# Attention into two MLP blocks on one core: P V of two heads in 128x64 tiles, row sums by their own products

## The chip, the core and the metric

The kernel runs on one core of a Trainium2 chip. TensorE (PE) does the products, VectorE (DVE) and ScalarE (ACT) the elementwise work, GpSimd (POOL) one reduction, and SyncE's queue (SP) issues the transfers. The metric is device time in microseconds (us); lower is better.

## The reference, cut to what is computed

```python
# q, k, v: 4 batches x 8 heads x 576 positions x 64
scores = scale * rotate(q) @ rotate(k).T
attn = exp(scores - max(scores)) ; attn /= sum(attn) + 1e-9
x = concat_heads(attn @ v)                                # 4 x 576 x 512
x = x + relu((x - mu) / sqrt(var + 1e-6) * g_ln @ w_ch1) @ w_ch2      # 512 -> 2048 -> 512
h = gelu(x @ w_in) ; u, v = split(h)                      # the second block
out = x + (u * (w_sg @ layernorm(v) + b_sg)) @ w_out
```

## The kernel before

All is float32. Products of weights and activations are split into a high and a low half and done as three single-pass products (`F32R`); P V, and the products with a matrix of ones, are done as plain `F32`, which the trace shows as two weight loads and two passes for each product.

**Attention** (class `Attn`) works in 64 units: 4 batches, 4 pairs of heads, 2 halves of 288 queries, 2 heads. A pair of heads of one half is a block (32 of them). Keys lie on the 128 partitions in 5 chunks, queries in the 288 columns. One unit (`unit`, L325) goes: scores S (10 products, L333) into the one five-bank PSUM tile; a maximum over the chunks on DVE (`mx`, L356); a maximum over the partitions on POOL (`am`, L359); then either `add` (L414: five products on PE add the negative maximum to S, and ACT takes the exponential out of PSUM) or `subtract` (L398: DVE subtracts from PSUM into SBUF, ACT takes the exponential there). P lies in `sT`, of which there are `SB` = 2. Then P V (L372, in the one PSUM bank `PV`): the stationary tile of 128 columns is 64 columns of V and 64 columns of ones, so one product gives P V in one half of the partitions and the row sums of P in the other. ACT copies both out (L379, L382), and a transfer brings one row of sums to `sums`. The first 31 units add; from the moment all 32 weight tiles are converted (`spare`, L485) every unit subtracts.

**Between and after**: `ln` (L495) divides by the sums and normalises when a batch's units are through; `rest` (L539) splits the result into `xh` and `xl`; `up` (L666) and `down` (L693) are the first MLP in four groups, one for each batch, 768 products a group; `moe2` (L923) is the second block. The 32 MLP weight tiles come as 8-byte values and are converted on ACT and DVE (`convert`, L636) during the first units.

**Order**: `Sched` (L61) places every step of every engine at build time, in a list for each engine, from a table of planned durations and ranks; the chip then runs these lists strictly in order, and only semaphores hold an engine up. So the table of durations decides the order and not the time.

Of the kernel before, what the change touches and what calls it, by code (L numbers as in the profile page):

```python
# [15 lines left out]
NC5 = 5  # L16
HQ = 288
SB, QB, KB, AB = 2, 3, 4, 1
WB, WX, CB = 8, 3, 4
KC = (0, 256, 576)  # L20
KEY0 = (0, 128, 256, 384, 448)
L_CONV = 10.0
HOLD = 0.4
UNIT = (0, 2.5, 2.5, 2.5)
# [107 lines left out]
class Attn:  # L132
# [10 lines left out]
    def __init__(self, tc, ctx, k, groups, sched):  # L143
# [7 lines left out]
        self.vin = [self.p.tile([128, NC5, 192], F32, tag=f"vin{i}", name=f"vin{i}", bufs=1) for i in range(2)]  # L151
        self.sums = [self.p.tile([64, HQ], F32, tag=f"sums{i}", name=f"sums{i}", bufs=1) for i in range(3)]
        self.last = {}
        self.done = []
        self.blocks, self.units = [], []
        for g, (b, halves) in enumerate(groups):
# [4 lines left out]
            for n, (hi, p) in enumerate(order):  # L161
# [6 lines left out]
                B["vof"]["users"] = B["vof"].get("users", 0) + 2  # L168
                B["kof"]["kusers"] = B["kof"].get("kusers", 0) + 2
                for j in range(2):  # L170
                    ends = j == 1 and (n == 7 or (g == 0 and n == 3))
                    self.units.append(dict(i=len(self.units), B=B, g=g, p=p, hi=hi, j=j, ends=ends))
# [38 lines left out]
    def first(self):  # L211
# [8 lines left out]
        t = self.p.tile([128, NC5, HQ], F32, tag="sT", name="q0", bufs=SB)  # L220
        self.sT.take()
# [27 lines left out]
    def prep(self, bi):  # L249
# [54 lines left out]
        if B["newk"]:  # L304
            c.task(k_task(), 3.01 + 0.02 * bi)
        c.task(*((q_twice(), 3.035) if bi == 1 else (q_task(), 3 + 0.02 * bi)))

    def load_v(self, bi):
        nc, B = self.nc, self.blocks[bi]

        def v_task():
            e = yield "SP", self.vfree.free, 0.7
            slot = B["vslot"] = self.vfree.take()
            t = B["vin"] = self.vin[slot]
            for j in range(2):
                if j:
                    e = yield "SP", 0.0, 0.7
                nc.sync.dma_start(out=t[:, :, 128 * j:128 * j + 64], in_=self.k["v"][B["b"], B["p"]][:, :, j, :])
            B["v"] = e + 5.5

        if B["newv"]:
            self.c.task(v_task(), 3.03 + 0.02 * bi)


    def unit(self, i):  # L325
# [34 lines left out]
        if self.k["spare"]():  # L360
# [3 lines left out]
        V = B["vof"]  # L364
        ps = None
        for c0, c1 in ((0, 2), (2, 5)):
            e = yield "PE", (lambda: latest(x1, self.PV.free(), V["v"])) if c0 == 0 else 0.0, 0.51 * (c1 - c0), 0.5
# [9 lines left out]
        a, b = 64 * j, 64 - 64 * j  # L377
        yield "ACT", e + 0.35, 0.41
        nc.scalar.copy(self.k["x0"](g, p, hi)[a:a + 64], ps[a:a + 64])  # L379
        e = yield "ACT", 0.0, 0.41  # L380
        t = self.p.tile([128, HQ], F32, tag="sr", name="sr", bufs=1)
        nc.scalar.copy(t[b:b + 32], ps[b:b + 32])  # L382
        self.PV.give(bank, e + 0.1)
        e = yield "SP", e + 0.1, 0.6
        r = 32 * hi + 2 * p + j
        nc.sync.dma_start(out=self.sums[self.sums_of(g, hi)][r:r + 1], in_=t[b:b + 1])
        if u["ends"]:
            self.done.append(e + 3.0)

    def new_sT(self):  # L390
        return self.sT.take(), self.p.tile([128, NC5, HQ], F32, tag="sT", name="sT", bufs=SB)

    def subtract(self, am, at):
# [7 lines left out]
        for c0, c1 in ((0, 2), (2, 5)):  # L401
            e = yield "ACT", e + 0.1 if c0 == 0 else 0.0, 0.1 + 0.29 * (c1 - c0)
# [3 lines left out]
    def add(self, am, at):  # L406
# [5 lines left out]
        for c0, c1 in ((0, 2), (2, 5)):  # L412
# [8 lines left out]
        c.e["ACT"] = max(c.e["ACT"], e + 0.35) + 0.89  # L421
# [24 lines left out]
def fused_kernel(ctx, tc, q, k, v, cs, cst, w12, wi, wo, wsg, wsg4, gb, out):  # L446
# [13 lines left out]
    ones = const.tile([128, 128], F32, name="ones")  # L460
    gbt = const.tile([128, 2, 4], F32, name="gbt")
# [23 lines left out]
    attn = Attn(tc, attn_ctx, dict(q=q, k=k, v=v, cs=csb, e=e128, x0=get_x0, x0_free=x0_free, spare=lambda: stored[0] == 32), groups, C)  # L485
# [9 lines left out]
    def ln(g, his, at):  # L495
        n = len(his)
        yield "DVE", at, 0.3
# [9 lines left out]
        for hi in his:  # L507
# [29 lines left out]
            C.task(rest(g, hi, his, st, xc, t, xn[0], e + 0.1), 2)  # L537
# [623 lines left out]
```

## Time and profile before

| | us |
|---|---|
| runs: median (lowest to highest of 3) | 973.72 (972.16 to 974.61) |
| profiled execution: span, first to last instruction | 970.5 |
| PE busy, products / weight loads | 924.1 / 857.2 |
| DVE busy | 705.4 |
| ACT busy | 470.0 |
| POOL busy | 87.8 |

The profiled execution is listed with its span alone; the runs lie 1.7 to 4.1 us above it, the median 3.2 us. The engines run side by side, so the busy times don't add up to the span. Products are pipelined on PE: a record lasts longer than the distance to the next one, and the cost of a product is the distance of two starts, not the length of the record.

### The profile page before, as it was taken

The numbers are of one execution on the slowest core, as the hardware profiler recorded it, in microseconds if no ns is written. First come the engines' busy times: TensorE is split into PE (matmuls) and PEld (weight loads), VectorE is DVE, ScalarE is ACT, GpSimd is POOL, SyncE is SP. The second block draws the span as 40 slices with busy tenths as digits, with TensorE's granted clock in tenths as the row PEclk, the third lists the DMA queues.
The fourth block names the chain that finished last, engine by engine and source line by source line (L and its number), as shares of the span: only waits on it lengthen the run. The fifth ranks groups of instructions, "written<-read, shape, count | busy, mean of one in ns | idle before, by whom it ended". The sixth has DMA issues, their size and how long they took to land.

```text
span 970.5 us, 15810 instructions
## 1 busy us (share of the span) xinstructions
PE 924.1 (95%) x6027; PEld 857.2 (88%) x6027; DVE 705.4 (73%) x1153; ACT 470.0 (48%) x946; POOL 87.8 (9%) x78
## 2 busy tenths in 40 slices
PE   4777899999999899999999999999999999999998
PEld 3555788999999789999989999999999999989998
DVE  6988766898878997678888744675543798677764
ACT  3666657776532464444245532525422467254431
POOL 1221111101110112120012110000000000000000
PEclk9998999999999999999999999999999999999999
DMA  8798733898537086564763723698753300303011
GB/s 228 207 276 269 222 85 87 249 333 279 185 126 217 14 209 188 163 196 119 237 185 92 221 92 110 221 301 259 245 194 110 92 8 12 98 1 93 1 49 50
DMA packets 93404, 153.47 MB, mean 158 GB/s; under 512 B 38032, under 2 KB 60816, under 8 KB 93328
## 3 DMA queue, kind: packets, MB, share of 16 engines
q1 hardware_dynamic: 92784, 151.86, 50.9%
q8 instruction: 48, 0.79, 0.3%
q10 hardware_dynamic: 544, 0.59, 0.2%
q14 instruction: 28, 0.23, 0.1%
HBM read 107.55 MB, written 26.21 MB: 138 GB/s over the span
## 4 chain that ended last, share of the span: by engine, by line
PE 81%; DVE 11%; DMA 3%; ACT 3%; issue 2%; POOL 1%; SPq 0%; DVEq 0%; ACTq 0%
PE PV L372 12%; PE S L333 7%; PE m L708 7%; PE m L707 7%; PE m L709 7%; PE m L677 6%; PE m L679 5%; PE m L678 5%; DVE mx L356 2%; DMA sums<-sr 2%; PE p L1072 2%; PE p L1070 2%; PE p L1071 2%; PE p L989 2%; PE p L988 2%; PE p L1087 2%
## 5 line engine op out<-in xcount | busy, mean ns | idle before, releaser
L372 PE MATMUL PV<-sT,vin 128*128 128x288 f32 x640 | 167.6, 409 | 1.1 <-ACT sr L382 0.9
L677 PE MATMUL m<-xh,w 128*128 128x288 f32 x480 | 147.8, 308 | 3.2 <-DVE h L687 3.2
L372 PEld LDWEIGHTS PV<-sT,vin 128*128 128x128 f32 x640 | 118.6, 191 | 29.0 <-ACT sr L382 1.4
L707 PE MATMUL m<-h,w 128*128 128x288 f32 x480 | 144.3, 301 | 0.0
L678 PE MATMUL m<-xl,w 128*128 128x288 f32 x480 | 142.6, 297 | 1.0 <-DVE xl L550 1.0
L679 PE MATMUL m<-xh,w 128*128 128x288 f32 x480 | 141.9, 296 | 0.0
L708 PE MATMUL m<-h,w 128*128 128x288 f32 x480 | 141.8, 296 | 0.0
L709 PE MATMUL m<-h,w 128*128 128x288 f32 x480 | 140.7, 293 | 0.0
L356 DVE TENSOR_REDUCE mx<-S 128x288 f32<-128x1440 f32 x64 | 105.9, 1655 | 39.6 <-PE S L333 37.2
L359 POOL PARTITION_ALL_REDUCE am<-mx x64 | 85.7, 1338 | 487.0 <-DVE mx L356 487.0
L333 PE MATMUL S<-X,K 128*128 128x288 f32 x640 | 111.8, 315 | 16.9 <-ACT X L202 9.6
L333 PEld LDWEIGHTS S<-X,K 128*128 128x128 f32 x640 | 93.4, 195 | 27.7 <-ACT sT L417 10.7
L687 DVE SCALAR_TENSOR_TENSOR h<-m,h 128x288 fp32r<-128x288 f32 x128 | 58.1, 454 | 63.9 <-ACT h L685 63.1
L685 ACT ACTIVATE h<-m 128x288 fp32r<-128x288 f32 x128 | 52.6, 411 | 98.8 <-PE m L679 98.0
L677 PEld LDWEIGHTS m<-xh,w 128*128 128x128 f32 x480 | 90.7, 189 | 7.3 <-DVE h L687 4.7
L678 PEld LDWEIGHTS m<-xl,w 128*128 128x128 f32 x480 | 90.9, 189 | 2.7 <-DVE xl L550 1.5
L707 PEld LDWEIGHTS m<-h,w 128*128 128x128 f32 x480 | 90.1, 188 | 1.2 <-DVE h L687 0.2
L708 PEld LDWEIGHTS m<-h,w 128*128 128x128 f32 x480 | 90.2, 188 | 1.0
L679 PEld LDWEIGHTS m<-xh,w 128*128 128x128 f32 x480 | 91.0, 190 | 0.0
L709 PEld LDWEIGHTS m<-h,w 128*128 128x128 f32 x480 | 90.1, 188 | 0.0
L379 ACT COPY x<-PV 64x288 f32<-64x288 f32 x64 | 25.2, 394 | 93.1 <-PE PV L372 92.6
L403 ACT ACTIVATE sT<-sT 128x576 f32<-128x576 f32 x66 | 50.9, 801 | 31.2 <-DVE sT L398 31.1
(151 smaller groups left out, 1855.7 us busy)
## 6 DMA issues: line engine op xcount, KB each, us to landing
w<-wsc SPq DMA_DIRECT2D x96, 512.0 KB, 4.5
X<-qin SPq DMA_DIRECT2D x120, 144.0 KB, 2.6
cd<-in_w SPq DMA_DIRECT2D x32, 512.0 KB, 5.9
wsc<-w SPq DMA_DIRECT2D x24, 512.0 KB, 4.4
kin<-in_k SPq DMA_DIRECT2D x15, 576.0 KB, 5.8
qin<-in_q SPq DMA_DIRECT2D x30, 288.0 KB, 4.4
vin<-in_v SPq DMA_DIRECT2D x40, 160.0 KB, 4.4
x1d<-x SPq DMA_DIRECT2D x32, 144.0 KB, 2.2
```

Source lines behind the costliest of these rows:

```text
L333: x = nc.tensor.matmul(S[:, ch, 0:HQ], Kb["K"][j][:, KEY0[ch]:KEY0[ch] + 128], B["X"][:, j, 1 - t, :], start=t == 0, stop=t == 1)
L356: nc.vector.tensor_reduce(mx, S[:, :, 0:HQ].rearrange("p c q -> p q c"), AX.X, ALU.max)
L359: nc.gpsimd.partition_all_reduce(am, mx, 128, bass_isa.ReduceOp.max)
L372: nc.tensor.matmul(ps, V["vin"][:, ch, 64 * j:64 * j + 128], sT[:, ch, :], start=ch == 0, stop=ch == 4)
L677: nc.tensor.matmul(ps, w[:, 0, ms], xh[:, kc, :], start=kc == 0, stop=False)
L678: nc.tensor.matmul(ps, w[:, 0, ms], xl[:, kc, :], start=False, stop=False)
L679: nc.tensor.matmul(ps, w[:, 1, ms], xh[:, kc, :], start=False, stop=kc == 3)
L685: G["relu"] = nc.scalar.activation(t[:, 0, :], ps, AF.Relu).ins
L687: nc.vector.scalar_tensor_tensor(t[:, 1, :], ps, 0.0, f32(t[:, 0, :]), op0=ALU.max, op1=ALU.subtract)
L707: nc.tensor.matmul(ps, w[:, 0, ms], t[:, 0, :], start=a == 0, stop=False)
L708: nc.tensor.matmul(ps, w[:, 1, ms], t[:, 0, :], start=False, stop=False)
L709: nc.tensor.matmul(ps, w[:, 0, ms], t[:, 1, :], start=False, stop=a == n - 1)
```

## The change

- **P V for two heads together.** `values` runs once for a block. The two heads' products have 64 stationary columns each (V alone) and go to the two halves of the partitions of the one PSUM tile, in turn: head 0, head 1, next chunk. It waits for both heads' exponentials.
- **Sums apart.** `norm` makes the row sums by products of 64 columns of ones with P, again for both heads in turn, into the bank `PV` after `values` has been copied out.
- **Chunks added on DVE.** `LEVEL` says for each block how far DVE adds the chunks of P before (`total`): level 0 none (5 products a head), 1 one addition of 128x576 (3 products), 2 also one of 128x288 (2 products), 3 also one of 64x288 (1 product). Blocks 0 to 15 and block 17 have level 0, two blocks level 1, four level 2 and nine level 3.
- **Copies and transfers.** ACT copies 128x288 twice a block, not 64x288 and 32x288 twice a unit; sums and V go by one transfer each where there were two.
- **Subtract or add** goes by a list (`TAKE`): 38 units subtract (33 before), 13 of them among the first 31 (none before); 26 units add (31 before).
- **Buffers and order.** `sT` has 3 tiles, and a fourth when the conversion's pool is closed; converted tiles have 3 load buffers, not 4. Ranks (`RANK`, `NORM`, `REST`, `UNIT`, `HOLD`) differ, so all lists differ up to the end of the third MLP group; from there PE's list is the same.

```diff
-SB, QB, KB, AB = 2, 3, 4, 1
-WB, WX, CB = 8, 3, 4
+SB, QB, KB, AB = 3, 3, 4, 1
+WB, WX, CB = 8, 3, 3
+LEVEL = [0, 0, 0, 0, 0, 0, 0, 0, 0, 0, 0, 0, 0, 0, 0, 0, 2, 0, 3, 1, 3, 2, 2, 3, 3, 3, 2, 3, 3, 3, 1, 3]
...
-        if self.k["spare"]():
+        if TAKE[i]:
             x1, slot, sT = yield from self.subtract(am, e)
         else:
             x1, slot, sT = yield from self.add(am, e)
-        V = B["vof"]
+        P = dict(at=x1, slot=slot, t=sT, left=2, end=0.0)
+        B["P"].append(P)
+        if B["level"]:
+            c.task(self.total(P, B["level"]), RANK["total"])
+        if j:
+            c.task(self.values(B), RANK["values"])
...
+    def total(self, P, level):
...
+        nc.vector.tensor_tensor(F, t[:, 0:2, :], t[:, 2:4, :], ALU.add)
+        if level > 1:
+            e = yield "DVE", 0.0, 0.47
+            nc.vector.tensor_tensor(F[:, 0, :], F[:, 0, :], F[:, 1, :], ALU.add)
+        if level > 2:
+            e = yield "DVE", 0.0, 0.47
+            nc.vector.tensor_tensor(F[64:128, 0, :], F[64:128, 0, :], t[64:128, 4, :], ALU.add)
...
+    def values(self, B):
...
             for ch in range(c0, c1):
-                nc.tensor.matmul(ps, V["vin"][:, ch, 64 * j:64 * j + 128], sT[:, ch, :], start=ch == 0, stop=ch == 4)
-        self.sT.give(slot, e)
+                for j in range(2):
+                    r = slice(64 * j, 64 * j + 64)
+                    nc.tensor.matmul(ps[r], V["vin"][:, ch, r], P[j]["t"][:, ch, :], start=ch == 0, stop=ch == 4)
...
+    def norm(self, B):
...
+        n = (5, 3, 2, 1)[level]
+        e = yield "PE", lambda: latest(self.PV.free(), *(x.get("Fat") for x in P)) if level else self.PV.free(), 0.1 + 0.49 * n
...
+        for i in range(n):
+            for j in range(2):
+                t, F = P[j]["t"], P[j].get("F")
+                tail = i == n - 1 and level < 3
+                x = t[:, 4, :] if tail else F[:, i, :] if level else t[:, i, :]
+                nc.tensor.matmul(ps[64 * j:64 * j + 64], one[:, int(tail), :], x, start=i == 0, stop=i == n - 1)
...
+        nc.sync.dma_start(out=self.sums[self.sums_of(B["g"], B["hi"])][r:r + 2], in_=t[0:128:64])
```

What stands in PE's list in the early units, scores to scores; the names behind K, sT and vin are tile numbers. Before, one head's P V follows the next unit's scores:

```order
L333 MATMUL S<-X,K_107 128x288 x10
L372 MATMUL PV<-sT,vin_81 128x288 x5
L414 MATMUL S<-am,e_63 128x288 x5
L333 MATMUL S<-X,K_165 128x288 x10
L372 MATMUL PV<-sT,vin_81 128x288 x5
L414 MATMUL S<-am,e_63 128x288 x5
```

Now, with ten products (L421, then L446) at each place of "...", of which the first two are shown:

```order
L342 MATMUL S<-X,K_171 128x288 x10
L421 MATMUL PV<-sT_83,vin_85 64x288
L421 MATMUL PV<-sT_84,vin_85 64x288
...
L493 MATMUL S<-am,e_63 128x288 x5
L342 MATMUL S<-X,K_172 128x288 x10
L446 MATMUL PV<-sT_83,one 64x288
L446 MATMUL PV<-sT_84,one 64x288
...
L342 MATMUL S<-X,K_228 128x288 x10
```

Both heads' P V now follow one unit's scores, and their sums follow the next unit's; in all there are 62 such groups of 64-column products, 50 of them after the 16th unit's scores, of which 25 are P V.

DVE's list where batch 1 is normalised (L516 and L522 divide and add up, L550 makes `xl`, which the MLP's second group waits for; L724 to L732 finish the first group's outputs). Before:

```order
L724 TENSOR_TENSOR acc<-m,acc 128x288
L730 TENSOR_TENSOR acc<-acc,rstd 128x288
L732 TENSOR_TENSOR x_921<-acc,x_921 128x288
L516 TENSOR_TENSOR x_2083<-ln,x_2083 128x288
L522 TENSOR_TENSOR lt<-lt,x_2083 128x288
L550 SCALAR_TENSOR_TENSOR xl<-xc,gbt,xh 128x288 x2
L516 TENSOR_TENSOR x_2501<-ln,x_2501 128x288
```

Now (L630 makes `xl`, L805 to L813 are the first group's outputs):

```order
L596 TENSOR_TENSOR x_1571<-ln,x_1571 128x288
L767 SCALAR_TENSOR_TENSOR h<-m,h 128x288
L630 SCALAR_TENSOR_TENSOR xl<-xc,gbt,xh 128x288 x3
L767 SCALAR_TENSOR_TENSOR h<-m,h 128x288
L630 SCALAR_TENSOR_TENSOR xl<-xc,gbt,xh 128x288
L602 TENSOR_TENSOR lt<-x_1200,x_1571 128x288
L767 SCALAR_TENSOR_TENSOR h<-m,h 128x288
L638 TENSOR_TENSOR lt<-xc 128x288
L638 TENSOR_TENSOR lt<-lt,xc 128x288
L805 TENSOR_TENSOR acc<-m,acc 128x288
```

`xl` stood behind the first group's last outputs and stands ahead of its last eight blocks of outputs now, with 96 or more MLP products of that group still to come on PE.

DVE's list in a unit of the second half, between two maxima. Before:

```order
L356 TENSOR_REDUCE mx<-S 128x288
L687 SCALAR_TENSOR_TENSOR h<-m,h 128x288
L204 TENSOR_TENSOR qin<-qin 128x288
L398 TENSOR_TENSOR sT<-S,am 128x1440
L687 SCALAR_TENSOR_TENSOR h<-m,h 128x288
L356 TENSOR_REDUCE mx<-S 128x288
```

Now:

```order
L365 TENSOR_REDUCE mx<-S 128x288
L217 TENSOR_TENSOR qin<-qin 128x288
L767 SCALAR_TENSOR_TENSOR h<-m,h 128x288
L400 TENSOR_TENSOR F<-sT_83 128x576
L767 SCALAR_TENSOR_TENSOR h<-m,h 128x288
L477 TENSOR_TENSOR sT_84<-S,am 128x1440
L767 SCALAR_TENSOR_TENSOR h<-m,h 128x288
L403 TENSOR_TENSOR F<-F 128x288
L406 TENSOR_TENSOR F<-F,sT_83 64x288
L400 TENSOR_TENSOR F<-sX_3095 128x576
L365 TENSOR_REDUCE mx<-S 128x288
```

The additions L400, L403 and L406 stand beside the maximum and the subtraction.

## Rows read from the trace of the kernel before

**Rows 1.** The page, part 1: engine, busy us (share of the span), instructions.

```profile
PE 924.1 (95%) x6027; PEld 857.2 (88%) x6027; DVE 705.4 (73%) x1153; ACT 470.0 (48%) x946; POOL 87.8 (9%) x78
```

**Rows 2.** The page, part 2: busy tenths and granted clock in 40 slices.

```profile
PE   4777899999999899999999999999999999999998
PEclk9998999999999999999999999999999999999999
```

**Rows 3.** Busy us by stretch: length, PE, PEld, DVE, ACT, POOL, clock, DMA.

```profile
0.00:121.00 121.00, 87.06 (x401) 67.36 (x402) 97.19 (x127) 72.02 (x132) 24.51 (x29) 0.97 0.81 241
121.00:277.00 156.00, 155.00 (x1008) 144.14 (x1008) 123.51 (x175) 99.83 (x191) 21.47 (x17) 1.00 0.64 199
277.00:330.00 53.00, 49.37 (x313) 45.14 (x311) 46.01 (x83) 19.83 (x41) 4.65 (x4) 0.97 0.44 138
330.00:700.00 370.00, 365.39 (x2463) 343.33 (x2462) 260.32 (x372) 165.57 (x332) 37.23 (x29) 1.00 0.60 184
```

**Rows 4.** Timeline of one early unit: start, us, engine, instruction [idle <-releaser].

```profile
54.38 1.85 PE L333 MATMUL S<-X,K 128*128 128x288 f32 x10 [0.35 <-ACT sT L417]
56.07 2.59 PE L372 MATMUL PV<-sT,vin 128*128 128x288 f32 x10
56.34 1.66 DVE L356 TENSOR_REDUCE mx<-S 128x288 f32<-128x1440 f32 x1
58.09 1.52 POOL L359 PARTITION_ALL_REDUCE am<-mx  x1 [5.04 <-DVE mx L356]
58.70 0.40 ACT L379 COPY x<-PV 64x288 f32<-64x288 f32 x1 [1.04 <-PE PV L372]
59.66 0.92 PE L414 MATMUL S<-am,e 128*128 128x288 f32 x5 [1.00 <-POOL am L359]
60.93 1.85 PE L333 MATMUL S<-X,K 128*128 128x288 f32 x10 [0.34 <-ACT sT L417]
```

**Rows 5.** The chain that ended last, one P V; start, us, what.

```profile
259.23 2.42 PE PV L372 x10
```

**Rows 6.** Timeline of PE where 64-column products stand between 128-column ones.

```profile
338.48 0.82 PE L333 MATMUL S<-X,K 128*128 128x288 f32 x5
339.23 0.70 PE L571 MATMUL ln<-lt,ones 128*64 128x288 f32 x2
339.86 0.40 PE L677 MATMUL m<-xh,w 128*128 128x288 f32 x1
340.10 0.29 PE L678 MATMUL m<-xl,w 128*128 128x288 f32 x1
340.23 0.29 PE L679 MATMUL m<-xh,w 128*128 128x288 f32 x1
```

**Rows 7.** L571's 64-column products: duration ns min/median/max, first and last start.

```profile
L571 PE MATMUL ln<-lt,ones x12: 406/432/457, 324.4 to 654.8; 128*64 128x288 f32 x12
```

**Rows 8.** Timeline of PE at the start of the MLP's second group.

```profile
317.31 0.40 PE L514 MATMUL ln<-rc,sel 128*128 128x288 f32 x1 [1.91 <-DVE x L516]
319.96 0.61 PE L678 MATMUL m<-xl,w 128*128 128x288 f32 x1 [0.62 <-DVE xl L550]
320.36 0.44 PE L679 MATMUL m<-xh,w 128*128 128x288 f32 x1
320.60 0.44 PE L677 MATMUL m<-xh,w 128*128 128x288 f32 x1
```

**Rows 9.** Groups by line and form on DVE: busy us, mean ns | idle before.

```profile
L356 DVE TENSOR_REDUCE mx<-S 128x288 f32<-128x1440 f32 x64 | 105.9, 1655 | 39.6 <-PE S L333 37.2 <-ACT xh L546 1.0 <-ACT qin L202 0.8
L398 DVE TENSOR_TENSOR sT<-S,am 128x1440 f32<-128x1440 f32 x33 | 54.4, 1648 | 15.1 <-POOL am L359 15.0
L178 DVE TENSOR_TENSOR qin<-qin,csb 128x576 f32<-128x576 f32 x32 | 24.2, 757 | 0.4 <-DMA qin<-in_q 0.2
L730 DVE TENSOR_TENSOR acc<-acc,rstd 128x288 f32<-128x288 f32 x32 | 14.9, 466 | 0.9
L506 DVE TENSOR_TENSOR rc<-sum,rc 64x288 fp32r<-64x288 f32 x5 | 2.3, 452 | 0.6 <-ACT rc L504 0.5
```

More of the change, by code (lines that the diff above doesn't have):

```diff
@@ L314, in v_task @@
             t = B["vin"] = self.vin[slot]
[L315 to L318, printed above, removed]
+            nc.sync.dma_start(out=t, in_=self.k["v"][B["b"], B["p"]].rearrange("p c j d -> p c (j d)"))
             B["v"] = e + 5.5
         if B["newv"]:
-            self.c.task(v_task(), 3.03 + 0.02 * bi)
+            self.c.task(v_task(), RANK["load"] + 0.02 * bi)
     def unit(self, i):
@@ L376, in unit, with more @@
             self.vfree.give(V["vslot"], e)
[L377 to L380, printed above, removed]
+        c.task(self.norm(B), RANK["sums"])
+        e = yield "ACT", e + 0.35, 0.41
+        nc.scalar.copy(self.k["x0"](B["g"], B["p"], B["hi"]), ps)
+        self.PV.give(bank, e + 0.1)
+        self.through(B, e + 0.1)
+    def norm(self, B):
+        nc, P, level = self.nc, B["P"], B["level"]
+        n = (5, 3, 2, 1)[level]
+        e = yield "PE", lambda: latest(self.PV.free(), *(x.get("Fat") for x in P)) if level else self.PV.free(), 0.1 + 0.49 * n
+        bank = self.PV.take()
+        ps = self.ps.tile([128, 512], F32, tag="PV", name="PV")[:, 0:HQ]
+        one = self.k["one"]
+        for i in range(n):
[4 more added lines that the diff above has]
+                nc.tensor.matmul(ps[64 * j:64 * j + 64], one[:, int(tail), :], x, start=i == 0, stop=i == n - 1)
+        for x in P:
+            self.leave(x, e + 0.1)
+            if level:
+                self.F.give(x["fslot"], e + 0.1)
+        e = yield "ACT", e + 0.35, 0.41
         t = self.p.tile([128, HQ], F32, tag="sr", name="sr", bufs=1)
-        nc.scalar.copy(t[b:b + 32], ps[b:b + 32])
+        nc.scalar.copy(t, ps)
         self.PV.give(bank, e + 0.1)
         e = yield "SP", e + 0.1, 0.6
[L385 to L388, printed above, removed]
+        r = 32 * B["hi"] + 2 * B["p"]
+        nc.sync.dma_start(out=self.sums[self.sums_of(B["g"], B["hi"])][r:r + 2], in_=t[0:128:64])
+        self.through(B, e + 3.0)
     def new_sT(self):
-        return self.sT.take(), self.p.tile([128, NC5, HQ], F32, tag="sT", name="sT", bufs=SB)
+        slot = self.sT.take()
+        return slot, self.sTt[slot]
+    def more(self, pool):
+        for n in range(SX):
+            self.sTt.append(pool.tile([128, NC5, HQ], F32, tag=f"sX{n}", name=f"sX{n}", bufs=1))
+            self.sT.at.append(0.0)
+        self.Fp = pool
+        self.F.at = [0.0] * FB
     def subtract(self, am, at):
@@ L849, in fused_kernel @@
     C.task(mlp(parts), 5)
-    C.run(lambda: over)
+    C.run(lambda: "norms" in over)
     attn_ctx.close()
     w2 = Weights2(tc, C, pctx.enter_context(tc.tile_pool(name="w2a", bufs=1, side="right")), wi, wo, wsg, wsg4)
+    if len(over) == 2:
+        last_group()
     C.task(ahead(), 4.5)
```

97 lines of the change are left out of this document (65 added, 32 removed).

## The prediction

> **What bounds the kernel now.** I read the busy times first: PE 924.1 of 970.5 us, DVE 705.4, ACT 470.0 [rows 1]. The slices then say when: PE is at 4 to 7 tenths in the first five and at 9 or nearly so from there on [rows 2]. The stretches give that in us. Up to 121 us, where the 16th unit's scores end, PE is busy 87.1 us; from 121 to 277 us 155.0 of 156; from 330 to 700 us 365.4 of 370; only from 277 to 330 us is it at 49.4 of 53.0 [rows 3]. So there are two regimes. In the first 121 us a unit is one serial round: scores at 54.38, maximum 56.34, POOL 58.09, the five products of `add` 59.66, next scores 60.93 [rows 4], 6.55 us, and P V (2.59 us as recorded) lies hidden beside the maximum and POOL. After 121 us PE's own work is the time: whatever is added to PE's list or taken from it counts in full, and work on DVE or ACT counts only if PE is made to wait.
>
> **Prices on PE.** One head's P V is 5 products in 10 passes and takes 2.42 us [rows 5]: 0.242 a pass, 0.484 a product. A 64-column product is no cheaper alone: its recorded duration is 406 ns at the least [rows 7], and the records in [rows 6] fit two passes of 0.242. So the change gains only if the two halves of the columns run at the same time, and no row of before shows that. What before does show is the price of going over to 64 columns and back [rows 6]. The last of five scores products starts at 338.48 + 4 x 0.13 = 339.00, and PE would be free for the next at 339.13; with 0.48 for the product of L571 and 0.13 for L677, L678 would start at 339.75. It starts at 340.10: about 0.34 us for the two changes of form. The Trainium skill (TensorEngine Tiling (Array Packing), Key Properties) says that changing the tiling mode drains the engine, and that different tiles can load weights and multiply in parallel; the first of these speaks against so many groups, and the row has its price; the second no run here shows.
>
> **The products, part by part.** After the 16th unit before still has 50 heads' P V: 50 x 2.42 = 121.0 us. The change has at the same place 25 P V groups of 5 pairs and 25 sums groups: ten of 5 pairs, two of 3, four of 2, nine of 1. That is 125 + 50 + 6 + 8 + 9 = 198 pairs. Side by side a pair costs one product, 0.484: 95.8 us. The 50 groups cost 50 x 0.34 = 17.0 us. That makes 112.8, a gain of 8.2. The list, however, is head 0, head 1, and each product is two passes on the same half of the columns: head 1's first pass can start at the earliest beside head 0's second, so that at the start of a group and at its end one half stands idle for a pass. In full that is 50 x 0.242 = 12.1 us and turns the gain into a loss of 3.9. No row shows two halves, so I take the middle: **-2.1 us, from -8.2 to +3.9**. Before the 16th unit the 12 groups stand beside the maximum and POOL: a P V group of 10 passes is 2.42 + 0.34 + at most 0.24 = 3.0 us, and between the scores' end (56.07) and `add` (59.66) there are 3.6 [rows 4]. If that cover went, 0.1 us a unit would cost little, and only halves that run one after the other (5.2 us) would cost much.
>
> **Subtract for add.** After the 16th unit 16 units add before and 16 now (the list's zeros from unit 16 on are 16; before it is units 15 to 30), so PE's list neither gains nor loses there. DVE gets 13 more subtractions among the first 31 units and 8 fewer after. Early on, five of the first 15 units change: `add` takes 59.66 to 60.93 = 1.27 us to the next scores, a subtraction 1.65 [rows 9] and a semaphore, some 0.45 more, but the scores after it need not wait for the second exponential (1.85 us recorded, with 0.3 of gaps). Net about 0.1 to 0.2 each, 1 us. The first batch's sums also come a unit later, after a second product. I take **+1 us, from -4 to +6**: the ends are about one serial round of 6.55 us up or down, since the lists differ and DVE is already busy 97.2 of 121 us there [rows 3].
>
> **The stall at 311 to 326 us.** PE waits 1.91 us for the division of batch 1 and 0.62 for `xl` [rows 8]; then the products start 0.24 apart (320.36, 320.60) where 0.13 is usual [rows 6]: the granted clock is at its lower level, 1.2 GHz, after PE had waited. The stretch loses 3.6 us idle and some 1.5 at the lower clock, 5.1 in all. The cause is the order on DVE: before, `xl` stands behind the first group's last outputs; now it stands ahead of eight of them, with some 96 products x 0.13 = 12.6 us of PE work between. So the wait should go, and nothing is late next, as the second half's normalisation has the first half's 96 products to hide behind. **-5 us, from -5 to 0.**
>
> **DVE.** The additions cost 30 x 0.757 (nearest row: `qin` 128x576) + 26 x 0.466 + 18 x 0.452 = 43.0 us, and the subtractions 5 x 1.648 = 8.2 [rows 9]; nearly all additions fall on units 34 to 63. In 277 to 700 us DVE was busy 46.0 + 260.3 = 306.3 of 423 [rows 3] and comes to 306.3 + 43.0 - 13.2 = 336, or 79%: not the bound. But its list is strict, a maximum and a subtraction of 1.65 each now have additions of 0.45 to 0.76 between them, and the next scores and the MLP's bank wait behind them. I take **+1.5 us of new waits on PE, from 0 to +8**.
>
> **Edits at nothing.** ACT loses 64 copies of 0.4 us [rows 4], and SP 52 transfers; neither is waited for in the saturated part. The sums' products need the bank `PV` after one copy of 0.40 us that starts at once when P V ends (58.66, 58.70) [rows 4]; at nearly all places 6 products or more (0.79) stand between, and without them it would be 0.5 us a block. The third and fourth `sT` let the scores of the next block go on while both heads wait for `values`; the third load buffer less for conversions costs nothing while conversions are through by unit 34, some 20 us before the second group needs them. PE's list from the end of the third MLP group on is unchanged.
>
> **Sum.** -2.1 + 1 - 5 + 1.5 = -4.6: a span of 965.9 for 970.5. The median of the runs lies 3.2 above the span; so **969.1 us** for 973.7, 0.5% faster. About 0.3%, or 2.9 us, is what a measurement of this kernel can tell from no change. With the ends of the terms this case runs from some 958 to 981.
>
> **Rivals.**
> *Weight loads don't get ahead (slower).* If the other half's weights can be loaded only once the product before them has started, each change of half shows the load: 457 against 406 ns where it lay bare, 0.05 us [rows 7]. A pair is then 0.484 + 2 x 0.05 = 0.586; 198 x 0.586 + 17.0 + 50 x 0.19 = 142.5, which is 21.5 over 121.0, and the time **993**. Every 0.01 us of bare load is 3.5 us of time, so it decides from about 0.01 on. For it: the heads alternate, so every product changes the half. Against it: in full-width lists loads never lie bare, with a product after every load. The Trainium skill (TensorE: Matmul & The Clock Gate, Part 3) has loads overlap running products only where the row groups differ, and both heads' tiles have all 128 rows; by that rule this is what would come.
> *The halves don't run together.* Then the change doesn't do what it says: 198 x 0.968 + 17.0 = 208.7, 87.7 over; and early 14 groups of 5.2 us in 3.6 us of cover, 22 more: **1,081**.
> *DVE's bursts hold the scores up (slower).* Ten units from unit 38 on hold 10 maxima, 9 subtractions, 12 + 11 + 4 additions and some 35 smaller steps, 71.5 us by the rows' durations; PE's list there comes to 81. It decides where such ten units take DVE over 95% of the time; at 0.4 us a unit for 32 units the time is **982**.
>
> **How the numbers follow.** Side by side, forecast: 0.70, and within it (centre -4.6, some 6 us either way) faster 0.43, same 0.20, slower 0.07. Bare loads: 0.12, slower. DVE: 0.12, slower. One after the other: 0.06, slower. Faster 0.43, same 0.20, slower 0.37. The likeliest case gives 969. The range goes from 957, a little under its low end, to 993, which takes in DVE's case and reaches the bare loads; it leaves out the serial case and the tails.
>
> **What would show it.** Right: in a P V group, 20 records with starts 2 every 0.24 us, some 2.7 us from first start to the next 128-column product's; PE at 9 tenths with no wait near 311 to 326 us and the clock at full there; L477's and L365's waits unchanged. Wrong: starts 0.29 apart twice a pair (bare loads), 0.24 for every record (serial), or idle PE in front of the scores with `sT<-S` as releaser (DVE). The forecast falls on the faster side if the group's idle passes are hidden, and on the slower one if a change of form costs over 0.45 us.

## The result, and the profile after

| us | before | after |
|---|---|---|
| runs: median (lowest to highest), 4 each, side by side | 973.66 (972.16 to 974.61) | 964.56 (963.86 to 967.19) |
| ratio of the times (95% interval) | | 0.9915 (0.9899 to 0.9931) |
| profiled execution: time; span | span 970.5 | 964.37; span 962.2 |

The change makes the kernel 0.9% faster: 964.6 us where 969.1 was forecast.

Parts 1 and 2 of the page of after, against [rows 1] and [rows 2]: busy us by engine, then PE's busy tenths and the granted clock in 40 slices.

```profile
PE 918.0 (95%) x6434; PEld 809.4 (84%) x6434; DVE 753.3 (78%) x1232; ACT 443.1 (46%) x882; POOL 89.2 (9%) x76
PE   3778899999999999999999999999999999999998
PEclk9998999999999999999999999999999999999999
```

PE has 407 more records and is busy 6 us less; DVE has 48 us more. The stretches of [rows 3] again, in after: length, PE, PEld, DVE, ACT, POOL, clock, DMA.

```profile
0.00:121.00 121.00, 84.21 (x472) 56.18 (x472) 99.67 (x126) 62.14 (x110) 24.32 (x27) 0.93 0.76 237
121.00:277.00 156.00, 154.47 (x1119) 126.03 (x1121) 136.77 (x178) 96.22 (x180) 22.48 (x18) 1.00 0.61 194
277.00:330.00 53.00, 52.20 (x380) 48.59 (x376) 46.66 (x87) 16.64 (x34) 3.82 (x3) 1.00 0.57 177
330.00:700.00 370.00, 368.23 (x2684) 329.77 (x2683) 291.57 (x446) 152.09 (x303) 38.60 (x29) 1.00 0.59 184
```

The first stretch has become worse: PE's granted clock has a mean of 0.93 there, where [rows 3] has 0.97. The third has lost its hole: 52.20 of 53 us busy for 49.37.

PE's timeline around one P V group of after: start, us, instruction. A single-pass product beside others of its kind takes 0.13.

```profile
236.19 0.29 PE L789 MATMUL m<-h,w 128*128 128x288 f32 x1
236.41 2.65 PE L421 MATMUL PV<-sT,vin 128*64 128x288 f32 x20
238.98 0.40 PE L787 MATMUL m<-h,w 128*128 128x288 f32 x1
239.22 0.30 PE L788 MATMUL m<-h,w 128*128 128x288 f32 x1
```

PE is free at 236.19 + 0.13 = 236.32. Without the group L788 would start one product later, at 236.45; it starts at 239.22. The group costs 2.77 us: ten passes of 0.242, which is 2.42, and 0.35 for the two changes of form. The 20 records start in pairs, 6 to 7 ns apart (236.406 and 236.413, 236.70 and 236.71, and so on, the last at 238.64). Both halves of the columns run side by side from the first pass to the last, and neither has an idle pass. So it is in 48 of the 50 groups after the 16th unit's scores. In two sums groups, at 358.5 and 432.1 us, the second head's passes start 0.52 and 0.16 us after the first's, and those groups last that much longer.

The weight loads of a sums group of after, beside its products:

```profile
51.75 2.14 PEld L446 LDWEIGHTS PV<-sT,one 128*64 128x64 f32 x20 [0.17 <-issue]
51.76 2.65 PE L446 MATMUL PV<-sT,one 128*64 128x288 f32 x20
```

The 20 loads end half a microsecond before the products do. Only the first load of each half starts together with its pass (236.405 and 236.406 us in the group above), and that pass is recorded with 457 ns, where all the others have 406. From the second pass on every load lies beside an earlier pass, though each product changes the half. The Trainium skill (TensorE: Matmul & The Clock Gate, Part 3) has loads overlap running products only where the row groups differ; both heads' tiles hold all 128 rows, and here they overlap. The trace decides against the rule for this case.

PE's timeline of after at the stall of [rows 8]:

```profile
319.52 0.29 PE L594 MATMUL ln<-rc,sel 128*128 128x288 f32 x1
319.65 0.29 PE L787 MATMUL m<-h,wx 128*128 128x288 f32 x1
...
323.51 0.30 PE L789 MATMUL m<-h,wx 128*128 128x288 f32 x1
323.65 0.30 PE L757 MATMUL m<-xh,w 128*128 128x288 f32 x1
323.78 0.29 PE L758 MATMUL m<-xl,w 128*128 128x288 f32 x1
```

The division's product (L594) and the first product with `xl` (L758) start 0.13 after the one before them. Nothing waits there, and the granted clock of the stretch is 1.00, the full 2.4 GHz.

What PE waited for in after, whole run: us in total, times, longest; the four largest.

```profile
PE S L342 <- ACT X L215: 10.5, 1, 10.5
PE S L342 <- DVE sT L477: 10.2, 4, 3.4
PE S L493 <- POOL am L368: 9.9, 5, 4.0
PE S L342 <- ACT sT L496: 2.2, 6, 0.4
```

The first is the kernel's start and stands in both. The others lie nearly all before 130 us.

**The account.** To add up the whole, I gave each product on PE its own step (0.131 single-pass, 0.22 for one of 512 columns, 0.242 a pass of `F32`, the two passes of a pair counted once) and called the rest of the distance between two starts a wait. From the end of the 16th unit's scores on, before has 849.4 us, of them 816.2 work and 29.9 waits (the rest is the last product's end and what follows). After has 837.2: 793.7 work, 50 x 0.354 = 17.7 for changes of form, and 22.3 waits. So the work is 22.5 less, the changes cost 17.7, the waits are 7.6 less: -12.2, but for rounding. Not all of these waits are idle time: undisturbed neighbours stand 0.1325 apart, and 0.234 with 512 columns, which makes some 10 us of either kernel's. Up to there after is 3.9 later (125.0 us for 121.1). Together that is -8.3, the difference of the spans.

### The profile page after: what moved, and what is told of

Read it like the earlier page. It is cut to its first block, busy times and chain, and to the rows that moved or that the text cites. A ratio compares the mean times of both kernels' runs of the same rounds, so it can differ in the third digit from the quotient of the medians.

```text
span 962.2 us, 16538 instructions
## 1 busy us (share of the span) xinstructions
PE 918.0 (95%) x6434; PEld 809.4 (84%) x6434; DVE 753.3 (78%) x1232; ACT 443.1 (46%) x882; POOL 89.2 (9%) x76
## 4 chain that ended last, share of the span: by engine, by line
PE 82%; DVE 10%; DMA 3%; issue 2%; ACT 2%; POOL 1%; SPq 0%; DVEq 0%; POOLq 0%
PE S L342 8%; PE PV L421 7%; PE m L757 7%; PE m L787 6%; PE m L759 6%; PE m L758 6%; PE m L788 6%; PE m L789 6%; PE PV L446 3%; DVE mx L365 3%; PE p L1157 2%; PE p L1155 2%; PE p L1156 2%; PE p L1074 2%; PE p L1073 2%; PE p L1172 2%
## 5 line engine op out<-in xcount | busy, mean ns | idle before, releaser
L757 PE MATMUL m<-xh,w 128*128 128x288 f32 x480 | 145.4, 303 | 0.6 <-DVE h L767 0.5
L788 PE MATMUL m<-h,w 128*128 128x288 f32 x480 | 141.9, 296 | 0.0
L758 PE MATMUL m<-xl,w 128*128 128x288 f32 x480 | 141.6, 295 | 0.0
L759 PE MATMUL m<-xh,w 128*128 128x288 f32 x480 | 141.2, 294 | 0.0
L342 PE MATMUL S<-X,K 128*128 128x288 f32 x640 | 109.4, 315 | 25.7 <-ACT X L215 10.5
L758 PEld LDWEIGHTS m<-xl,w 128*128 128x128 f32 x480 | 90.2, 188 | 0.4
L788 PEld LDWEIGHTS m<-h,w 128*128 128x128 f32 x480 | 90.2, 188 | 0.3
L421 PE MATMUL PV<-sT,vin 128*64 128x288 f32 x560 | 88.5, 427 | 0.0
L421 PEld LDWEIGHTS PV<-sT,vin 128*64 128x64 f32 x560 | 44.2, 143 | 32.3 <-issue 7.8
L482 ACT ACTIVATE sT<-sT 128x576 f32<-128x576 f32 (+1 forms) x62 | 47.4, 800 | 26.0 <-DVE sT L477 25.8
L477 DVE TENSOR_TENSOR sT<-S,am 128x1440 f32<-128x1440 f32 x31 | 51.2, 1651 | 7.5 <-PE PV L446 3.8
```

What stands on the lines that cost most here:

```text
L342: x = nc.tensor.matmul(S[:, ch, 0:HQ], Kb["K"][j][:, KEY0[ch]:KEY0[ch] + 128], B["X"][:, j, 1 - t, :], start=t == 0, stop=t == 1)
L421: nc.tensor.matmul(ps[r], V["vin"][:, ch, r], P[j]["t"][:, ch, :], start=ch == 0, stop=ch == 4)
L757: nc.tensor.matmul(ps, w[:, 0, ms], xh[:, kc, :], start=kc == 0, stop=False)
L758: nc.tensor.matmul(ps, w[:, 0, ms], xl[:, kc, :], start=False, stop=False)
L759: nc.tensor.matmul(ps, w[:, 1, ms], xh[:, kc, :], start=False, stop=kc == 3)
L788: nc.tensor.matmul(ps, w[:, 1, ms], t[:, 0, :], start=False, stop=False)
```

## The experiments

All ratios are to the kernel before, run on the same chip beside them. "Work" and "waits" are those of the account.

**1. One head after the other within a group.** Both loops over products are turned round (`values`, and `norm` in the same way):

```diff
-            for ch in range(c0, c1):
-                for j in range(2):
+            for j in range(2):
+                for ch in range(c0, c1):
```

> One edit: in the P V and in the sums products of a pair of heads, all of head 0's products come first and then all of head 1's, where they alternate in the changed kernel (964.6 us). In the changed kernel's trace both halves of the columns start within 7 ns of each other, pass by pass, and five pairs take 2.42 us. Theory A, PE takes its list in order and only neighbours in the list run side by side: of ten products at most one overlaps, so a group of five pairs takes some 4.4 + 0.35 us, 1.9 more; 35 such groups after the 16th unit are 68 us, the shorter ones some 4, and early 4.7 us no longer fit in 3.6 us of cover, some 15 more: 1,045 to 1,060 us. Theory B, each half has a queue of its own and runs ahead of the list: no change, 963 to 967 us.

Measured: 994.5 us, 1.0225 (1.0204 to 1.0246). A sums group in PE's timeline of this kernel:

```profile
233.92 0.29 PE L789 MATMUL m<-h,w 128*128 128x288 f32 x1
234.14 4.15 PE L446 MATMUL PV<-sT,one 128*64 128x288 f32 x20
238.22 0.40 PE L787 MATMUL m<-h,w 128*128 128x288 f32 x1
```

From first start to the next form this group takes 4.08 us; the P V group above takes 2.57 (236.41 to 238.98). Neither one after the other (twice as long) nor as before. The starts of this group's 20 records tell why: head 0's first six passes start alone, at 0, 0.29, 0.54, 0.78, 1.02 and 1.26 us; its seventh starts at 1.506 and head 1's first at 1.512; four passes of each run side by side, and head 1's last six run alone. So PE does not take its list strictly in order here, as was said of the kernel before: it starts products on the other half some four passes ahead of their place, and in this run no more. P V, issued in two steps of two and three chunks, takes 3.11. Ten full sums groups at 1.5 us more and 25 P V groups at 0.53 make 28 us; measured is +29.9 against after. Neither theory came. Without the alternation there is no gain, and "the halves don't run together" is refuted.

**2. No additions on DVE.**

```diff
-LEVEL = [0, 0, 0, 0, 0, 0, 0, 0, 0, 0, 0, 0, 0, 0, 0, 0, 2, 0, 3, 1, 3, 2, 2, 3, 3, 3, 2, 3, 3, 3, 1, 3]
+LEVEL = [0, 0, 0, 0, 0, 0, 0, 0, 0, 0, 0, 0, 0, 0, 0, 0, 0, 0, 0, 0, 0, 0, 0, 0, 0, 0, 0, 0, 0, 0, 0, 0]
```

> One edit: level 0 for every block, so DVE adds no chunks and every sums group has five pairs. Theory, PE's products are the time after the 16th unit: 52 pairs more x 0.484 = 25 us, so 989 to 991 us, slower than the kernel before (973.7), since two heads side by side and sums apart save nothing by themselves: 50 pairs of five for 50 heads, and 50 groups x 0.35 us on top. Rival, DVE's additions (43 us) cost PE waits that go as well: 978 to 985 us.

Measured: 992.0 us, 1.018 (1.016 to 1.020): +27.4 against after, where 52 pairs x 0.484 = 25.2 were reckoned; the theory is right and its range ends 1 us too low. This sets apart what the change gains by. Without the additions the 50 groups have 250 pairs, 121.0 us, just what before's 50 heads' P V had: a pair of half-width P V products and a pair of half-width sums products take together as long as before's two full-width products, which made P V and sums in one. Two heads side by side save nothing by themselves, and the changes of form make that version slower than before. All of the gain on PE's products is the 52 pairs that DVE's additions take away.

**3. All additions in every block from the 17th on.**

```diff
-LEVEL = [0, 0, 0, 0, 0, 0, 0, 0, 0, 0, 0, 0, 0, 0, 0, 0, 2, 0, 3, 1, 3, 2, 2, 3, 3, 3, 2, 3, 3, 3, 1, 3]
+LEVEL = [0, 0, 0, 0, 0, 0, 0, 0, 0, 0, 0, 0, 0, 0, 0, 0, 3, 3, 3, 3, 3, 3, 3, 3, 3, 3, 3, 3, 3, 3, 3, 3]
```

> One edit: level 3 for all of blocks 16 to 31 (nine of them have it in the changed kernel). Theory, PE's products are the time: 12 pairs fewer x 0.484 = 5.8 us, so 958 to 960 us. Rival, DVE is at its limit there (10.6 us more additions in strict order between maxima and subtractions): 964 to 970 us, with idle PE ahead of the scores.

Measured: 975.6 us, 1.0022 (1.0008 to 1.0037). PE's work fell by 6 us, as reckoned, but its waits rose by 17. Two of them, from what PE waited for in this kernel, then its row for 330 to 700 us:

```profile
PE p L1171 <- ACT w L1140: 3.7, 1, 3.7
PE p L1125 <- DVE xl L1061: 2.5, 1, 2.5
...
330.00:700.00 370.00, 363.43 (x2638) 326.54 (x2637) 299.66 (x462) 150.29 (x300) 39.97 (x29) 1.00 0.59 183
```

DVE is only 8 us busier there than in after, yet PE is idle 4.8 us more there, and in the second MLP block it waits for the normalised `v` (`w`, L1140) and for `xl`. After those waits the clock is at its lower level for 3.4 and 6.8 us. The theory is refuted. The rival has the right sign, but the time lies above its 964 to 970, and the two longest new waits are not in front of the scores, where it expected them. This run doesn't say whether the additions or the lists planned anew made them.

**4. DVE's room, measured with the lists kept.** Experiment 3 plans all lists anew, so two more runs leave each step in its place. In one, each addition takes in 16 of 288 columns, and the other columns are left out of the sums; in the other, the blocks of levels 1 and 2 get all three additions, issued behind the first one.

```diff
-        nc.vector.tensor_tensor(F, t[:, 0:2, :], t[:, 2:4, :], ALU.add)
+        nc.vector.tensor_tensor(F[:, :, 0:16], t[:, 0:2, 0:16], t[:, 2:4, 0:16], ALU.add)
... (the other two additions likewise)
```

> The changed kernel with the same lists on every engine, but the additions of P's chunks on VectorE (60 or so instructions from the 33rd unit on, 43 us by the rows of the kernel before) take in only 16 of the 288 columns, so that each costs perhaps 0.1 to 0.15 us in place of 0.45 to 0.76; the other columns of the sums are left out of the result. Product for product PE does the same. Theory: VectorE's additions lie beside PE's work and are waited for only in part; of the 22 us of waits on PE after the 16th unit's scores the additions make 2 to 5, so the time falls to 960 to 963 (965 is what the changed kernel gives). Rival: the waits that are left on PE (scores that wait for a subtraction, a subtraction that waits for a sums product to free its tile) are the additions' doing, and most of them go: 950 to 956. Second rival: the additions cost nothing, since the waits have other releasers: 964 to 966.

```diff
         if level > 1:
             e = yield "DVE", 0.0, 0.47
-            nc.vector.tensor_tensor(F[:, 0, :], F[:, 0, :], F[:, 1, :], ALU.add)
+        nc.vector.tensor_tensor(F[:, 0, :], F[:, 0, :], F[:, 1, :], ALU.add)
... (the third addition likewise)
         one = self.k["one"]
+        if level:
+            n, level = 1, 3
```

> The changed kernel with its lists kept as they are and only the additions raised: the two blocks of level 1 and the four of level 2 get all three additions (level 3), each issued behind the block's first one without being planned for, so that no step changes its place on any engine; their sums are one pair of products in place of three or two. PE has 2 x 2 + 4 x 1 = 8 pairs fewer, 8 x 0.484 = 3.9 us; VectorE has 4 x 0.47 + 12 x 0.45 = 7.3 us more, spread over six blocks between the 33rd and the 63rd unit. Theory (VectorE has room for them as long as the lists stay, since the additions cost next to nothing when they are cut to 16 columns, and what cost 17 us where the level was raised with the planner's knowledge was the new lists): 960.5 to 963. Rival (VectorE's stretches were full and the additions made the waits there): 965 to 972.

Measured: 963.8 us, 0.9903 (0.9879 to 0.9928), with 16 columns, and 963.3, 0.9895 (0.9874 to 0.9916), with the levels up. Both intervals overlap that of after (0.9899 to 0.9931). DVE's additions by form, in after and then with 16 columns: busy us, mean ns | idle before.

```profile
L400 DVE TENSOR_TENSOR F<-sT 128x576 f32<-128x576 f32 x23 | 18.1, 785 | 3.3 <-ACT sT L496 2.4 <-PE PV L446 0.9
L403 DVE TENSOR_TENSOR F<-F 128x288 f32<-128x288 f32 x26 | 14.3, 551 | 0.5
L406 DVE TENSOR_TENSOR F<-F,sT 64x288 f32<-64x288 f32 x14 | 6.7, 476 | 0.5
```
```profile
L403 DVE TENSOR_TENSOR F<-F 128x16 f32<-128x16 f32 x26 | 5.7, 219 | 0.5
L400 DVE TENSOR_TENSOR F<-sT 128x32 f32<-128x32 f32 x23 | 4.6, 198 | 5.1 <-PE PV L446 2.6 <-ACT sT L499 2.4
L406 DVE TENSOR_TENSOR F<-F,sT 64x16 f32<-64x16 f32 x14 | 3.8, 269 | 0.5
```

With all forms (those from `sX` too) the additions take 46.6 us in after and 16.4 with 16 columns. 30 us less on DVE change neither the time nor the waits (39.8 us, changes of form among them, for 40.0): at their present number the additions cost next to nothing. What shows of a cost is 0.7 us, in the two sums groups whose heads start apart; with 16 columns the heads start together there too. The second rival (964 to 966) is nearest. One short addition takes 0.2 to 0.27 us, not the expected 0.1 to 0.15.

With the levels up the result stands between theory and rival. In the profiled execution, the slowest of its six, PE's work is 3.9 us less and its waits 6.7 more. In three of the six raised sums groups the second head starts late, and they last 1.0, 1.3 and 2.1 us from first start to the next form, where other one-pair groups last 0.64. Two of PE's waits there (after has 0.9 in two for the first, and no such row as the second):

```profile
PE S L342 <- DVE sX L479: 3.2, 2, 2.8
PE PV L448 <- DVE F L406: 0.8, 1, 0.8
```

So in that execution some of the raised additions came too late for their sums. The median of the six is 1.2 us under that of after, too little to tell from it: whether DVE still has room in these blocks stays open. Since six of experiment 3's seven raised blocks are raised here too, the larger part of its 17 us of waits belongs to the lists planned anew.

**5. What a change of form costs.** In the middle of each of the P V groups one 128-column product is put in, with only 64 moving columns. It starts a sum of its own in the bank in the middle of P V's, so this kernel is there for its time alone.

```diff
+            if c0:
+                nc.tensor.matmul(full[:, HQ:HQ + 64], self.k["e"], self.k["sel"][:, 0, 0, 0:64], start=True, stop=True,
+                                 skip_group_check=True)
```

> The changed kernel with one more product in the middle of each P V group, 128 columns stationary and 64 moving, into columns of the same bank that nothing reads; the planned durations and so all lists are otherwise the same. Theory, each going over to 64 columns and back costs 0.35 us: 25 groups after the 16th unit x (0.35 + 0.03 to 0.06) = 10 us, so 973 to 976 us, with the early ones hidden. Rival, the price is one of waiting for data at the group's start, not of the form: 25 x 0.06 = 1.5 us, 965 to 967 us.

Measured: 971.2 us, 0.9986 (0.9973 to 0.9999), 6.7 us over after. PE's timeline of one group:

```profile
237.32 1.19 PE L425 MATMUL PV<-sT,vin 128*64 128x288 f32 x8
238.44 0.30 PE L420 MATMUL PV<-sel,e 128*128 128x64 f32 x1
238.67 1.68 PE L425 MATMUL PV<-sT,vin 128*64 128x288 f32 x12
240.27 0.40 PE L791 MATMUL m<-h,w 128*128 128x288 f32 x1
```

From 237.32 to 240.27 are 2.95 us, 0.38 more than the 2.57 of after. 25 such groups after the 16th unit make 9.5, and the stretch after it became 7.6 us longer. Less the added product's own 64 columns (some 0.03, as 288 take 0.13), a change of form costs 0.35 us there and back, as in the groups of after, and waiting for data at a group's start is ruled out. The time itself stayed 2 us under the theory's 973 to 976.

**6. The early clock.** Six products that nothing reads, after each P V and each sums group of the first seven blocks, keep PE busier:

```diff
+        if B["n"] < 7:
+            t = self.k["mps"].tile([128, 512], F32, tag="m", name="fill")[:, 0:HQ]
+            for _ in range(6):
+                self.nc.tensor.matmul(t, self.k["e"], self.k["sel"].rearrange("p a b m -> p (a b m)")[:, 0:HQ], start=True, stop=True)
```

> The changed kernel with six products that nothing reads (128x288, into a bank that is unused by then) after each P V and each sums group of the first seven blocks; all else in the lists is the same. Theory, the early part is lengthened by the lower clock, which PE is granted after stretches with little work (five stretches of 3.4 us up to 121 us): with 0.8 us more work in each round there are fewer of them, the 16th unit's scores end 2 to 4 us sooner (at 121 to 123 us), and the time is 961 to 963.5 us. Rival, the six products hold up the addition of the maximum by some tenths of a us in each round and the clock stays as it is: 965 to 969 us.

Measured: 967.3 us, 0.994 (0.992 to 0.996). Busy by stretch, 40 to 100 us, first after, then this kernel; the clock stands after POOL's column.

```profile
40.00:60.00 20.00, 15.28 (x84) 10.06 (x86) 18.81 (x23) 13.58 (x24) 3.70 (x3) 0.85 0.84 266
60.00:80.00 20.00, 15.30 (x93) 9.86 (x90) 17.90 (x23) 12.24 (x23) 4.48 (x3) 0.89 0.87 289
80.00:100.00 20.00, 15.88 (x97) 9.71 (x97) 18.11 (x22) 10.65 (x20) 4.50 (x3) 0.91 0.90 292
```
```profile
40.00:60.00 20.00, 16.91 (x104) 11.60 (x104) 18.62 (x23) 12.74 (x22) 4.17 (x3) 0.91 0.78 246
60.00:80.00 20.00, 16.99 (x108) 11.61 (x104) 17.91 (x23) 12.43 (x23) 4.48 (x3) 0.91 0.91 299
80.00:100.00 20.00, 17.59 (x120) 12.21 (x120) 18.81 (x23) 11.78 (x22) 4.49 (x3) 1.00 0.94 303
```

The clock falls three times in place of five, each time for 3.4 us, and over the six runs its mean is 0.991 to 0.995, where after's four have 0.985 to 0.991. Still the 16th unit's scores end at 127.1, 2.1 later, and the time is 2.7 us longer: the products cost more than the clock gives back. The theory is right about the clock, the rival about the time.

**7. Adding instead of subtracting in the first 16 units.**

```diff
-TAKE = [0, 0, 0, 1, 0, 0, 0, 1, 0, 1, 0, 0, 1, 0, 1, 1, ...
+TAKE = [0, 0, 0, 0, 0, 0, 0, 0, 0, 0, 0, 0, 0, 0, 0, 0, ...
```

> One edit: the first 16 units all add on PE (six of them subtract on DVE in the changed kernel, whose 16th unit's scores end at 125.0 us where they end at 121.1 us before). Theory A, the subtractions lengthen the serial round by 0.8 us each: the 16th scores end at some 121 us and the time is 959 to 962 us. Theory B, the early loss is from two groups of products for each block and the lower clock that PE is granted more often there (five stretches of 3.4 us up to 121 us, one of 6.8 before): no change, 963 to 967 us.

Measured: 980.8 us, 1.0078 (1.0065 to 1.0091). Neither theory came. The 16th unit's scores end at 124.3 for 125.0; executions with after's own early lists end between 121.9 and 125.5 (below), so one profile doesn't tell what the subtractions cost there; the 4 us that theory A expected don't show. The 16 us come later, from other lists: waits after the 16th unit rise by some 12 us, and 5 us of products and changes of form are still to come that after has behind it by then. PE waits in this kernel for POOL's maximum 14 times, where after has 5:

```profile
PE S L493 <- POOL am L368: 22.1, 14, 4.0
```

**8. The ranks, each way.** Before gets after's ranks, and after gets before's:

```diff
-HOLD = 0.4
-UNIT = (0, 2.5, 2.5, 2.5)
+HOLD = 0.3
+UNIT = [-1, 1.25, 1, 1]
+RANK = dict(convert=3, end=0.5, prep=3, load=2.75, loader=2.75)
+NORM, REST = [1.25, 3, -1, 4], [1, 1.75, 1, 1.25]
```

> The kernel before, with the changed kernel's ranks alone (HOLD, UNIT, RANK, NORM, REST); products, subtractions and buffers are as before. Theory, the wait of PE at 311 to 326 us went by the order alone: about 5 us less than before (973.7), 967 to 970 us, and no wait of PE at the start of the MLP's second group. Rival, these ranks suit only the changed work, and other waits come: 974 to 985 us.

> The changed kernel with the ranks of the kernel before (HOLD, UNIT, RANK, NORM, REST); those that are new (for P V, sums and additions) stay. Theory, products and order each bring their part: the products' part stays (some 8 us after the 16th unit) and the waits come back, 968 to 976 us. Rival, the order carries all of it: 976 us or more.

Measured: 990.7 us, 1.018 (1.016 to 1.020), for before with the new ranks, and 990.1, 1.0175 (1.015 to 1.020), for after with the old ones. Work on PE after the 16th unit is that of the kernel each stems from; the waits are some 44 us for 29.9, and 66.1 for 40.0 (the changes of form among them). First two waits of the one, then in PE's timeline the other's longest but for that of the kernel's start:

```profile
PE PV L374 <- DVE xc L536: 2.8, 1, 2.8
PE PV L374 <- DVE x L518: 2.1, 1, 2.1
```
```profile
319.92 0.61 PE L787 MATMUL m<-h,w 128*128 128x288 f32 x1 [7.74 <-ACT w L737]
```

In the one P V waits for a normalisation to give up the PSUM bank, in the other the MLP for a converted weight. The rivals are right both times, the first even beyond its range (974 to 985): either half of the change alone is 17 us slower than before, both together 9 faster.

**9. Two single numbers of the planner.** Before with the second batch's attention set ahead of the MLP, and after with another `HOLD`:

```diff
-UNIT = (0, 2.5, 2.5, 2.5)
+UNIT = (0, 1.25, 2.5, 2.5)
```

> The kernel before with one rank changed (that of the second batch's units, from 2.5 to 1.25, so that its attention stands ahead of the first MLP's). No product is added or taken away. Theory: the stall at 311 to 326 us (3.6 us idle and 1.5 at the lower clock) was a matter of where batch 1's normalisation stood in VectorE's list, and this rank moves it: the stall goes and nothing as large takes its place, 967 to 970. Rival: any other rank plans all lists anew, and lists whose ranks weren't chosen together come out with waits elsewhere, as with the other two exchanges of ranks (990 each): 975 to 995.

```diff
-HOLD = 0.3
+HOLD = 0.4
```

> The changed kernel with one planner's constant (HOLD) at 0.4 in place of 0.3: the same work, the same list of levels and of subtractions, other lists. Theory (the work is worth -8 us and the rest of the order is luck of a few us either way): 962 to 972. Rival (the changed kernel's lists are a narrow optimum, as the exchanged ranks suggest): 975 to 990, that is no faster than before at all.

Measured: 970.5 us, 0.9972 (0.9959 to 0.9985), and 977.4, 1.0036 (1.0019 to 1.0054). PE's timeline of the first at the stall:

```profile
320.03 0.40 PE L514 MATMUL ln<-rc,sel 128*128 128x288 f32 x1 [1.90 <-DVE x L516]
320.27 0.29 PE L677 MATMUL m<-xh,w 128*128 128x288 f32 x1
320.40 0.29 PE L678 MATMUL m<-xl,w 128*128 128x288 f32 x1
```

The wait for `xl` and the lower clock of [rows 8] are gone; the wait for the division stays. That is worth some 3 us, as much as the kernel gained, and not the whole 5; the theory is right, half a microsecond beside its range. In the second, one number gives new waits on PE:

```profile
PE ln L594 <- DVE xc L614: 3.5, 1, 3.5
...
PE PV L421 <- DVE xc L614: 2.1, 1, 2.1
```

The same work is then slower than before. There the rival (a narrow optimum) is right.

## Why the prediction was right, and where it wasn't

The time lies in the range (957 to 993) and the direction is right, but the gain is nearly twice the forecast one: -8.3 us of span where -4.6 was reckoned. That it came this near is in part luck: the products were taken 5.4 us too dear and the early part 5.6 us too cheap.

| term | forecast | measured | by |
|---|---|---|---|
| products after the 16th unit | -2.1 (-8.2 to +3.9) | -7.5 | P V group of after; 1, 2, 5 |
| up to the 16th unit | +1 (-4 to +6) | +3.9 in time, +2.7 in work left for later | account; much of the 3.9 goes with the clock |
| stall at 311 to 326 us | -5 (-5 to 0) | about -5 | timeline of after; 9 |
| new waits for DVE | +1.5 (0 to +8) | the other waits fell by 2.6 | account; 4 |

- **The price of a pass and of a change of form** held: 0.242, and 0.35 for the reckoned 0.34.
- **The idle pass at each group's ends** is the step that was wrong. "Head 1's first pass can start at the earliest beside head 0's second" took the list's order for the order of starts. The two heads' first passes start 7 ns apart, and experiment 1 shows PE four passes ahead on the other half. The 12.1 us that the middle value took half of are nil: 95.8 + 17.7 - 121.0 = -7.5, near the low end.
- **Bare weight loads** and **serial halves** are refuted by the group's 20 records. The 457 ns that the prediction read as a bare load come once on each half of a group, and not at each change of half.
- **The stall** went, for the reason given: `xl` is there in time. Experiment 9 shows that a rank alone removes the `xl` part of it without any of the new products.
- **DVE's bursts** did not come: the additions took 46.6 us for the reckoned 43.0 and cost next to no time (experiment 4). But the reason is the list that was chosen: levels raised with lists planned anew lose 17 us to waits (experiment 3).
- **The early part** was sized too small. It is 3.9 us later, and 2.7 us of work is still to come that before has behind it by then: 8 passes of a normalisation (1.9) and 6 products of the MLP (0.8). Much of the 3.9 goes with the clock. The kernels of experiments 2, 3 and 4 have after's lists on every engine up to the 16th unit's scores, and yet these end at 121.9, 122.7, 125.5 (16 columns) and 124.8 us (levels up), with the clock at its lower level, from its first rise on, for 10.2, 10.2, 13.7 and 17.1 us up to there; after has 125.0 and 17.1, before 121.1 and 6.8. Against experiment 2's execution (its first stretch stands below) after falls back by 0.5, 0.8 and 1.3 us across its three further stretches at the lower level (from 57.6, 88.3 and 112.2 us), which is 2.6 of the 3.1 between them. Before's early lists ended at 121.1 us and, in experiment 9's first kernel, which keeps them too, at 122.9, with 6.8 us at the lower level both times. So what the early lists themselves cost can't be read from one execution of each kernel. That the clock falls more often with after's lists is not an accident of one execution: its mean is 0.985 to 0.991 in after's four runs, and 0.991 to 0.998 in 17 runs of before, beside experiment 1. Why it does stays open; experiment 6 shows that it rises with more products on PE, which cost more than they bring.
- **The assumption under all terms**, that lists not named in the sum are as good after as before, was luck. Exchanged ranks move the time by 17 to 26 us either way, one constant by 13. The 2.6 us by which the other waits fell belong to this planning; no run shows an edit of the products that brings them. The third `sT`, the list of subtractions after the 16th unit and the wider copies were not tried by themselves either.
- **Slips in the working**: the ends of the terms add up to 957 and 992 us, not to 958 and 981; the fifth of the early slices in [rows 2] stands at 8 tenths; and the early groups are 14, as under the serial halves, where the cover was worked out for 12 (two P V groups are followed by their sums with nothing between). None of these moves the forecast.

The first stretch of [rows 3] in experiment 2, which has after's lists there. The clock is 0.96, and 0.93 in after:

```profile
0.00:121.00 121.00, 82.62 (x496) 55.12 (x496) 102.58 (x129) 64.07 (x115) 24.44 (x27) 0.96 0.78 239
```

None of the kernels run is faster than after beyond what can be told apart; the one with the levels up in experiment 4 has the lowest median, 963.3. A version with a fourth `sT` tile in the early part, where two heads are held at once, was not run.

## What to carry to other kernels

Two half-width products side by side take as long as one full-width product, and what they replace here already used its full width for two results; count passes before and after, over everything that the old product made. The gain came from sums taken off PE onto an engine with room, less 0.35 us for each change of form, the same for a short group and a long one, so few long groups should beat many short ones. In a kernel whose lists come from a planner, a change of work and its new ranks have to be tried together: each alone was slower than before, and a wait that appears in a trial run is often the planner's and not the edit's.

## What the runs showed of the hardware

- Two 128x64 `F32` products on the two halves of the columns start 6 to 7 ns apart and run pass by pass at 0.242 us. From the second pass on their weight loads are hidden, although both hold all 128 rows (the P V group of after).
- Products on one half start up to four passes (1 us) ahead of their place in PE's list when that half is free; for the others they wait (experiment 1: six passes alone, four together, six alone).
- The change from 128 to 64 columns and back costs 0.35 us on PE, and 0.38 with a single short 128-column product between, that product's own time included (experiment 5). It doesn't depend on the group's length: in after a group of 2 passes a head takes 0.64 us from its first start to the next form and one of 10 takes 2.58, which is 0.242 a pass more.
- In the early units, where PE waits in each round, the granted clock falls to 1.2 GHz: up to the 16th unit's scores once, for 6.8 us, in before, and five times, for 3.4 us, in after. Executions of the same early lists differ in it, with 10.2 to 17.1 us at the lower level and up to 3.6 us in time. At that level a pass takes 0.48 us for 0.242. The 20 records of this P V group run at it until 47.36 us and last 3.81, for 2.65 at full clock:

```profile
44.98 3.81 PE L421 MATMUL PV<-sT,vin 128*64 128x288 f32 x20
```
